# A mixer block with MLP: which engine measures, transposes and orders the first tiles of x

## The chip, the cores and the metric

The kernel runs on one core of one Trainium2 chip. A core has a matrix engine (TensorE, PE in the profile; PEld is its weight load), a vector engine (VectorE, DVE), a scalar engine (ScalarE, ACT), GpSimd (POOL) and a queue engine (SyncE, SP) that issues DMA transfers. The engines run their own instruction streams in order and wait for each other through semaphores. The metric is the device time of one execution in microseconds (us), lower is better; the median of three runs stands for the kernel.

## The reference

```python
B, S, D, F = 1, 2048, 512, 1792          # bf16; w1, w2: D x D; w3: D x F; w4: F x D
def reference(x, w1, w2, w3, w4):
    h = _gelu(_layernorm(x, axis=-1) @ w1)
    c = D // 4
    g0 = jnp.pad(h[:, :, 0*c:1*c], ((0, 0), (1, 0), (0, 0)))[:, :S, :]
    g1 = jnp.pad(h[:, :, 1*c:2*c], ((0, 0), (0, 1), (0, 0)))[:, 1:, :]
    g2 = jnp.pad(h[:, :, 2*c:3*c], ((0, 0), (2, 0), (0, 0)))[:, :S, :]
    g3 = jnp.pad(h[:, :, 3*c:   ], ((0, 0), (0, 2), (0, 0)))[:, 2:, :]
    hs = jnp.concatenate([g0, g1, g2, g3], axis=-1) @ w2
    x1 = x + hs
    h2 = _gelu(_layernorm(x1, axis=-1) @ w3) @ w4
    return x1 + h2
```

Four quarters of the channels of h are shifted along the sequence by 1, -1, 2 and -2 before the second product.

## The kernel before

The 2048 rows are 16 tiles of 128 rows. Row 16p + t lies in tile t, on partition p, so that a shift by one row is, for nearly all rows, a step to the neighbouring tile. The work of a tile of x in the first layer is:

- `st` (line 325, VectorE): statistics of 128x512; `ag` (328, VectorE): mean and variance from them
- `rs` (POOL): a shift of the variance by epsilon (line 349) and a power of -1/2 (358), mostly for two tiles at once
- `norm` (378, VectorE): the normalized tile, `xn`
- the transpose to `xT`: either `tp` (400, four 128x128 transposes on TensorE into PSUM) and then `evA` (412, the eviction by ScalarE), or `dT` (388), one DMA transpose issued by SP. Tiles 0 to 7 go the first way, tiles 8 to 15 the second
- the first product, for pairs p of tiles: pair 0 by input chunk (`m1i`, line 467: 16 matmuls of 256 columns, four chunks of w1 in four steps, so that the first half of w1 is enough to begin), the others by output chunk (`m1`, 451: four matmuls of 256 columns a step)
- `g1` (495, 501, 512, ScalarE): GELU of a pair, into `hT`
- the second product of a tile (`m2`, 526): four matmuls of 512 columns, one for each shifted quarter j, which needs the quarter's neighbouring tile; `add` (538, VectorE) gives x1.

The second layer measures and normalizes tiles of x1 in the order 2, 3, ..., 15, 0, 1 (these are numbers 16 to 31 in the helpers), transposes all of them by DMA (`x1T`), and runs the third product (553) and the fourth (579) in four blocks of 512 rows; a DVE add (593) and a DMA write each output tile.

Every engine's instruction stream is in program order. The order of the first layer's head is written out by hand in the string `HEAD`, whose steps are recorded one after the other (`m1 2 0 3` is pair 2, into PSUM bank 0, output chunk 3; `m2 2 4 0 1` is tile 2, bank 4, quarters 0 and 1; `tp 1 5` is tile 1 into bank 5). The helper then derives the semaphore waits from what each operation reads and writes. An operation that waits holds up all that stands behind it on its engine. The code behind `HEAD` records the rest with helpers for two tiles at a time.

SP issues, in this order: x tiles 0, 1, 2, 3 singly, 4 and 5 together, w1 in two halves, tiles 6 and 7, 8 to 11, 12 to 15, w2, the eight DMA transposes of tiles 8 to 15, w3, twelve transposes of x1, and then w4 in four pieces between the last four. PSUM has eight banks; a step that writes a bank waits until the bank's previous reader is done. Twelve matmuls on constants run at the start and three more when tile 1's statistics are there (`warm`, line 611); they compute nothing that is used.

Of the kernel before, what the change touches and what calls it, by code (L numbers as in the profile page):

```python
# [167 lines left out]
norm 10; g1 3; m2 3 5 0 1 2 3; st 14; ag 12; dT 9; rs 12; st 15; m2 4 6 0 1 2 3; ag 14; ag 15;  # L168
m1 4 0 3; rs 14; dT 11; m1 4 0 1; norm 13; m1 4 0 0; add 3; norm 14; dT 10; m2 5 7 0 1 2 3;
add 2; m1 4 0 2; norm 12; norm 15; dT 13; g1 4; dT 12; dT 14; dT 15  # L170
"""


def bass_standalone__mixer_s_mlp__prompt_kernel(
# [26 lines left out]
    with ExitStack() as es:  # L201
        sb = lambda name, shape, dt: es.enter_context(nc.sbuf_tensor(name, shape, dt))
        x_sb = sb("x_sb", [P, NT, D], BF16)
        x1_sb = sb("x1_sb", [P, NT, D], BF16)
        xT = sb("xT", [P, DC, S], BF16)
# [7 lines left out]
        ident = sb("ident", [P, P], BF16)  # L213
        xn = sb("xn", [P, NXN, D], BF16)
# [14 lines left out]
        pr = Prog()  # L229
# [38 lines left out]
        def load_w4(c, n):  # L268
            g = Gen()
            g_w4.append(g)  # L270
            v = w4.rearrange("(c p) f -> p c f", p=P)
            pr.op("sp", f"w4_{c}", lambda e: e.dma_start(w4_sb[:, c : c + n, :], v[:, c : c + n, :]),
                  w=[g], dma=True)


        def consts():
            g0 = Gen()
            pr.op("pool", "ident0", lambda e: e.memset(ident[:], 0.0), w=[g0])
            g_ident.prev = g0
# [26 lines left out]
        def window(j, t):  # L306

            s = (-1, 1, -2, 2)[j]
            u = t + s
            if 0 <= u < NT:  # L310
                return pos(j, u), [g_h[(j, u // 2)]]
            v = u % NT
            pads = [g_pad[k] for k in g_pad if k in PADS and k[0] == j]
            return pos(j, v) + (-1 if s < 0 else 1), [g_h[(j, v // 2)]] + pads


        def src(q):
# [13 lines left out]
        g_sd = {}  # L331

        def rstd_act(q, n=1):
            g = g_sd[q] = Gen()
# [10 lines left out]
        def rstd_pool(q, n=2, shift=False):  # L345
# [15 lines left out]
            if shift:  # L361
# [2 lines left out]
                                                rstd[:, q : q + n], ALU.mult),  # L364
                      r=[gm] + g_rstd[q : q + n], w=g_nmr[q : q + n])

        def norm(eng, q):
            a, g = src(q)
            s = q % NXN
            g_xn[q] = xn_slot[s].new()  # L370
            if eng == "act":
                pr.op("act", f"norm{q}",
                      lambda e: e.activation(xn[:, s, :], a, ACT_F.Identity,  # L373
                                             bias=nmr[:, q : q + 1], scale=rstd[:, q : q + 1]),
                      r=[g, g_nmr[q], g_rstd[q]], w=[g_xn[q]])
            else:
                pr.op(eng, f"norm{q}",
                      lambda e: e.tensor_scalar(xn[:, s, :], a, mv[:, q, 0:1], rstd[:, q : q + 1],  # L378
                                                ALU.subtract, ALU.mult),
                      r=[g, g_mv[q], g_rstd[q]], w=[g_xn[q]])  # L380
# [25 lines left out]
        def evacT(eng, q):  # L406
            g, b = g_tp[q]
            dst, c = xT_of(q)
            a = ps_bf[:, 1024 * b : 1024 * b + 512].rearrange("p (c s) -> p c s", c=DC)
            o = dst[:, :, P * c : P * (c + 1)]  # L410
            if eng == "act":
                pr.op("act", f"ev{q}", lambda e: e.activation(o, a, ACT_F.Copy), r=[g], w=[g_xT[q]])  # L412
            else:
                pr.op("dve", f"ev{q}", lambda e: e.tensor_copy(o, a), r=[g], w=[g_xT[q]])
# [44 lines left out]
        def mm1_by_input(p, b, dcs):  # L459

            if p not in g_y:
                g_y[p] = ([bank[b + i].new() for i in range(DC)], b)
            for dc in dcs:
                def f(e, dc=dc):
                    for fc in range(DC):
                        dst = ps[:, 512 * (b + fc) : 512 * (b + fc) + 256]
                        ins = e.matmul(dst, w1_sb[:, dc, P * fc : P * (fc + 1)],
                                       xT[:, dc, 256 * p : 256 * (p + 1)],
                                       start=(dc == 0), stop=(dc == DC - 1))
                    return ins  # L470

                pr.op("pe", f"mm1_{p}_1_{dc}", f,
                      r=[g_w[("w1", dc)], g_xT[2 * p], g_xT[2 * p + 1]], w=g_y[p][0])

        def hap(j, p, jn=1):

# [36 lines left out]
                      r=gens, w=[g_h[(j, p)] for j in range(DC)])  # L513


        g_o = {}

        def mm2(t, b, js=(0, 1, 2, 3)):

            if t not in g_o:  # L520
                g_o[t] = (bank[b].new(), b)
            win = [window(j, t) for j in js]

            def f(e):
                for j, (c, _) in zip(js, win):
                    ins = e.matmul(bankap(b), hT[:, j, c : c + P], w2_sb[:, j, :],  # L526
                                   start=(j == 0), stop=(j == DC - 1))
# [76 lines left out]
        def keep_warm(n, b, after=()):  # L604

            g = bank[b].new()
            ones = nc.const_aps.tensor(1.0, (P, 512), BF16)

            def f(e):
                for _ in range(n):  # L610
                    ins = e.matmul(bankap(b), ones[:, 0:P], ones, start=True, stop=True)  # L611
                return ins

            pr.op("pe", f"warm{len(after)}", f, r=list(after), w=[g])
# [37 lines left out]
        def mm2s(k, b):  # L652
            for i in range(2):
                mm2(ORDER2[k + i], b + i)
# [31 lines left out]
        def last_tile():  # L686
# [6 lines left out]

        steps = {
            "st": stats, "ag": aggr, "rs": rstd_pool, "norm": lambda q: norm("dve", q), "tp": peT,
            "evA": lambda q: evacT("act", q), "dT": dmaT,
            "m1i": lambda p, b, *dcs: mm1_by_input(p, b, dcs),
            "warm": lambda n, b, q: keep_warm(n, b, [g_mv[q]]),
            "m1": lambda p, b, *fcs: mm1(p, b, fcs), "g1": gelu1,
            "m2": lambda t, b, *js: mm2(t, b, js), "add": add1,  # L700
        }
# [73 lines left out]
```

## Time and profile before

| what | value |
|---|---|
| median of 3 runs | 138.96 us (138.89 to 139.28) |
| the profiled execution, its own time | 139.09 us |
| its span, first to last instruction | 137.3 us |
| TensorE busy | 131.9 us, 96% of the span |
| VectorE busy | 51.6 us |
| ScalarE busy | 50.0 us |
| POOL busy | 18.3 us |
| first transpose on TensorE | 6.76 us |
| first product (pair 0) | 8.73 us |
| first matmul of the second layer | 38.03 us |
| TensorE's granted clock | 1.00 throughout |

Busy times are summed from the records of single instructions. TensorE's matmuls overlap in the pipeline, and the ends of their records are modelled, so its share says little about idle moments: these are read from the starts of successive matmuls. In a timeline row stand the start, the busy time, engine and line, operation, output and input, shape and count, and in brackets the idle time before it with what ended it.

### The profile page before, as it was taken

The page shows a single profiled execution, that of the slowest core. Times are in us where ns is not written, and L with a number is a line of the kernel's source. Part 1 is how long each engine was busy: PE and PEld are TensorE (multiplying, and loading weights), DVE is VectorE, ACT ScalarE, POOL GpSimd, SP SyncE. Part 2 cuts the span into 40 slices and gives each one's busy share as a digit, 9 for nine tenths or more (in the row PEclk, how much of TensorE's full clock was granted, in tenths as well). Part 3 has the DMA queues.
Part 4 walks back from the last instruction along what each step waited for, and adds up shares of the span by engine and source line. Part 5 has one row for each costly group of instructions (what it writes and reads, how often), then busy time and mean ns, then how long its engine had stood idle before and what let it go on. Part 6 is the DMA issues. An engine that isn't in the chain of part 4 may idle for free.

```text
span 137.3 us, 1790 instructions
## 1 busy us (share of the span) xinstructions
PE 131.9 (96%) x689; PEld 66.5 (48%) x701; DVE 51.6 (38%) x125; ACT 50.0 (36%) x60; POOL 18.3 (13%) x52
## 2 busy tenths in 40 slices
PE   7879999999999999999999999999999999999993
PEld 3267847664444444444444444444444444444452
DVE  0989899999976620000232000023200002232222
ACT  4068622399545555552000555300055530000000
POOL 2542442464312200000000000000000000000000
PEclk9999999999999999999999999999999999999999
DMA  4996144589955599300111100011110001111121
GB/s 106 289 283 238 27 93 82 111 261 351 133 100 113 83 287 257 103 5 0 38 38 38 38 0 5 0 38 38 38 38 0 5 0 38 38 38 38 38 74 41
DMA packets 20119, 12.16 MB, mean 89 GB/s; under 512 B 13712, under 2 KB 19088, under 8 KB 20112
## 3 DMA queue, kind: packets, MB, share of 16 engines
q1 hardware_dynamic: 19968, 12.03, 33.6%
q8 instruction: 5, 0.08, 0.3%
q10 hardware_dynamic: 144, 0.03, 0.1%
q14 instruction: 2, 0.02, 0.0%
HBM read 6.82 MB, written 2.10 MB: 65 GB/s over the span
## 4 chain that ended last, share of the span: by engine, by line
PE 83%; DVE 8%; DMA 4%; POOL 1%; issue 1%; DVEq 0%
PE ps L579 35%; PE ps L553 35%; PE ps L526 8%; PE ps L451 5%; DVE st L325 5%; DVE xn L378 2%; DMA x_sb<-in_x_dram 2%; DMA xT<-xn 2%; POOL rstd L358 1%; DVE mv L328 1%; POOL vpe L349 0%; DVE o_sb L593 0%; DVEq L134 0%
## 5 line engine op out<-in xcount | busy, mean ns | idle before, releaser
L579 PE MATMUL ps<-w_sb,h2T 128*128 128x512 bf16 (+2 forms) x234 | 48.7, 366 | 0.2
L553 PE MATMUL ps<-x1T,w_sb 128*128 128x512 bf16 x219 | 48.6, 379 | 0.3
L566 ACT ACTIVATE h2T<-ps 128x1024 bf16<-128x1024 f32 x28 | 28.6, 1023 | 44.8 <-PE ps L553 44.8
L593 DVE TENSOR_TENSOR o_sb<-ps,x_sb 128x512 bf16<-128x512 f32 (+2 forms) x17 | 11.2, 660 | 75.0 <-PE ps L579 75.0
L579 PEld LDWEIGHTS ps<-w_sb,h2T 128*128 128x128 bf16 x238 | 22.8, 98 | 25.9
L553 PEld LDWEIGHTS ps<-x1T,w_sb 128*128 128x128 bf16 x224 | 21.9, 98 | 26.4
L325 DVE BATCH_NORM_STATS2 st<-x_sb 128x6 f32<-128x512 bf16 x32 | 20.7, 675 | 2.3 <-DMA x_sb<-in_x_dram 2.3
L526 PE MATMUL ps<-w_sb,hT 128*128 128x512 bf16 x61 | 14.3, 379 | 0.2
L451 PE MATMUL ps<-xT,w_sb 128*128 128x256 bf16 x112 | 14.0, 273 | 0.3 <-DMA xT<-xn 0.3
L451 PEld LDWEIGHTS ps<-xT,w_sb 128*128 128x128 bf16 x112 | 10.6, 98 | 3.1 <-issue 0.7
L358 POOL TENSOR_TENSOR rstd<-vpe,neghalf 128x2 f32<-128x2 f32 (+1 forms) x17 | 11.8, 695 | 1.0
L538 DVE TENSOR_TENSOR x_sb<-ps,x_sb 128x512 bf16<-128x512 f32 x16 | 10.3, 678 | 0.3 <-PE ps L526 0.2
L378 DVE TENSOR_SCALAR xn<-x_sb,mv,rstd 128x512 bf16<-128x512 bf16 x22 | 8.3, 405 | 5.2 <-POOL rstd L358 5.0
L526 PEld LDWEIGHTS ps<-w_sb,hT 128*128 128x128 bf16 x64 | 6.2, 98 | 6.3 <-ACT hT L512 0.3
L373 ACT ACTIVATE xn<-x_sb,nmr,rstd 128x512 bf16<-128x512 bf16 x10 | 7.6, 807 | 3.3 <-POOL nmr L363 3.3
L512 ACT ACTIVATE hT<-ps 128x1024 bf16<-128x1024 f32 x6 | 6.1, 1019 | 6.1 <-PE ps L451 6.0
L349 POOL TENSOR_SCALAR vpe<-mv 128x2 f32<-128x2 f32 (+1 forms) x17 | 3.9, 229 | 27.3 <-DVE mv L328 27.2
L412 ACT ACTIVATE xT<-ps 128x512 bf16<-128x512 bf16 x8 | 4.5, 603 | 5.9 <-PE ps L400 5.9
L611 PE MATMUL ps<-const-bfloat16-1.0 128*128 128x512 bf16 x15 | 5.4, 522 | 0.9 <-PEq L760 0.8
L328 DVE BATCH_NORM_AGGREGATE mv<-st 128x2 f32<-128x6 f32 x32 | 4.9, 172 | 0.1
L400 PE MATMUL ps<-ident,xn 128*128 128x128 bf16 x32 | 3.0, 221 | 1.2 <-DVE xn L378 1.2
L611 PEld LDWEIGHTS ps<-const-bfloat16-1.0 128*128 128x128 bf16 x15 | 1.8, 127 | 4.0 <-issue 3.2
(18 smaller groups left out, 12.8 us busy)
## 6 DMA issues: line engine op xcount, KB each, us to landing
w_sb<-in_w_dram SPq DMA_DIRECT2D x4, 512.0 KB, 4.8
out_dram<-o_sb SPq DMA_DIRECT2D x15, 128.0 KB, 1.8
w_sb<-in_w_dram SPq DMA_DIRECT2D x1, 1792.0 KB, 7.3
x_sb<-in_x_dram SPq DMA_DIRECT2D x2, 512.0 KB, 7.5
w_sb<-in_w_dram SPq DMA_DIRECT2D x3, 256.0 KB, 4.1
x_sb<-in_x_dram SPq DMA_DIRECT2D x4, 128.0 KB, 2.5
x_sb<-in_x_dram SPq DMA_DIRECT2D x2, 256.0 KB, 4.1
x1T<-xn SPq DMA_TRANSPOSE x16, 3.6
```

The lines of the kernel that those rows point to most:

```text
L325: pr.op("dve", f"st{q}", lambda e: e.bn_stats(st6[:, q, :], a), r=[g], w=[g_st[q]])
L358: lambda e: e.tensor_tensor(rstd[:, q : q + n], vpe[:, q : q + n], neghalf[:, 0:n], ALU.pow),
L373: lambda e: e.activation(xn[:, s, :], a, ACT_F.Identity, bias=nmr[:, q : q + 1], scale=rstd[:, q : q + 1]),
L378: lambda e: e.tensor_scalar(xn[:, s, :], a, mv[:, q, 0:1], rstd[:, q : q + 1], ALU.subtract, ALU.mult),
L451: ins = e.matmul(dst, w1_sb[:, dc, P * fc : P * (fc + 1)], xT[:, dc, 256 * p : 256 * (p + 1)], start=(dc == 0), stop=(dc == DC - 1))
L526: ins = e.matmul(bankap(b), hT[:, j, c : c + P], w2_sb[:, j, :], start=(j == 0), stop=(j == DC - 1))
L538: lambda e: e.tensor_tensor(x1_sb[:, t, :], bankap(b), x_sb[:, t, :], ALU.add),
L553: ins = e.matmul(bankap(b + i), w3_sb[:, dc, P * fc : P * (fc + 1)], x1T[:, dc, 512 * s : 512 * (s + 1)], start=(dc == 0), stop=(dc == DC ...
L566: pr.op("act", f"g2_{s}_{fp}", lambda e: e.activation(o, a, ACT_F.Gelu_apprx_tanh), r=gens, w=[g])
L579: ins = e.matmul(ps[:, 512 * b : 512 * b + n], h2T[:, fc, s % 2, P * i : P * (i + 1)], w4_sb[:, fc, c0 : c0 + n], start=(fc == 0), stop=(f ...
L593: lambda e: e.tensor_tensor(o_sb[:, s, 0:n], ps[:, 512 * b : 512 * b + n], x1_sb[:, t, c0 : c0 + n], ALU.add),
L611: ins = e.matmul(bankap(b), ones[:, 0:P], ones, start=True, stop=True)
```

## The change

- x tiles 6 and 7 are transposed by DMA, as the first two of now ten transposes of the first layer on SP's queue; their two `tp` and two `evA` are gone.
- Tile 2's statistics come from ScalarE in two passes that sum along the row, `sum` (x) and `dev` ((x - mean) squared), with small POOL steps for the negated mean, for the shifts of tiles 2 and 3 (`vpd`, `vp`) and for the joint power (`pw`). Its `st` and `ag` are gone from VectorE.
- Tile 0 is normalized and transposed first, behind the statistics of tiles 0, 1 and 3; tile 5 is measured between norms 0 and 1. The three later `warm` matmuls stand behind the transpose of tile 0, and eleven instead of twelve lead.
- Pair 0 of the first product goes tile by tile (`m1x`: 32 matmuls of 128 columns instead of 16 of 256).
- Second products of tiles 2 to 7 are recorded as single matmuls, a quarter at a time, in an order of their own between the first products; the first one issued opens the sum and the last closes it, whichever quarter it is.
- Two memsets of constants go from POOL to VectorE; w4 is loaded in two pieces instead of four.

```diff
 HEAD = """
-st 0; ag 0; rs 0 1; st 1; ag 1; rs 1 1; st 2; st 3; ag 2; ag 3; warm 3 3 1; rs 2; norm 1; norm 0;
-tp 1 5; tp 0 4; st 4; evA 1; norm 2; norm 3; evA 0; tp 2 6; tp 3 7; st 5; ag 4; ag 5; m1i 0 0 0;
-evA 3; rs 4; m1i 0 0 1; evA 2; m1i 0 0 2; st 6; m1i 0 0 3; norm 4; m1 1 4 3; norm 5; g1 0;
-tp 4 6; st 7; m1 1 4 0; ag 6; ag 7; tp 5 7; rs 6; evA 4; m1 1 4 1; st 9; evA 5; m1 1 4 2; st 8;
-norm 7; m1 2 0 1; ag 8; ag 9; g1 1; m1 2 0 3; rs 8; norm 6; tp 7 7; st 11; m1 2 0 2; evA 7;
-tp 6 6; norm 8; m1 2 0 0; ag 11; evA 6; m2 2 4 0; m2 2 4 1; st 10; m1 3 2 2; norm 9; ag 10; g1 2;
-m1 3 2 0; rs 10; st 13; m1 3 2 1; m1 3 2 3; st 12; m2 2 4 2; dT 8; m2 2 4 3; norm 11; ag 13;
...
+st 0; ag 0; rs 0 1; st 1; sum 2; st 3; ag 1; ag 3; rs 1 1; norm 0; tp 0 4; dev 2; vpd 2; vp 3;
+evA 0; st 5; warm 3 3 1; norm 1; pw 2 2; tp 1 5; st 4; m1x 0 0 0; ag 5; m1x 0 0 1; norm 3; evA 1;
+m1x 0 0 2; norm 2; ag 4; tp 3 7; m1x 0 0 3; rs 4; m1x 1 0 0; st 6; evA 3; tp 2 6; m1x 1 0 1;
+m1x 1 0 2; st 7; ag 6; evA 2; m1x 1 0 3; ag 7; rs 6; norm 4; g1 0; m1 1 4 0; norm 5; tp 4 6;
+m1 1 4 2; tp 5 7; norm 6; evA 4; m1 1 4 3; evA 5; st 9; m1 1 4 1; st 8; m1 2 0 3; ag 9; ag 8;
+rs 8; m1 2 0 0; norm 7; g1 1; m1 2 0 2; st 13; m1 2 0 1; m2 3 5 0; st 11; m2 2 4 0; dT 6; norm 8;
+m2 5 7 2; m2 2 4 1; g1 2; m2 2 4 2; st 10; ag 11; m2 3 5 2; ag 10; m2 3 5 1; rs 10; norm 9;
+m2 4 6 2; dT 7; m2 5 7 0; m2 2 4 3; st 12; m1 3 2 1; m2 4 6 0; st 14; m2 3 5 3; norm 11; ag 13;
+dT 8; m1 3 2 3; add 2; m1 3 2 2; norm 10; ag 12; m1 3 2 0; ag 14; m2 6 4 2; rs 12; dT 9;
+m2 4 6 1; m2 6 4 0; st 15; ag 15; g1 3; m1 4 0 0; rs 14; m1 4 0 2; norm 13; m2 6 4 1; dT 11;
...
 """
-            pr.op("pool", "eps", lambda e: e.memset(eps_c[:], LN_EPS), w=[g_eps])
-            pr.op("pool", "nh", lambda e: e.memset(neghalf[:], -0.5), w=[g_nh])
+            pr.op("dve", "eps", lambda e: e.memset(eps_c[:], LN_EPS), w=[g_eps])
+            pr.op("dve", "nh", lambda e: e.memset(neghalf[:], -0.5), w=[g_nh])
...
+        def sum_act(q):
...
+            pr.op("act", f"sq_sum{q}",
+                  lambda e: e.activation(sink[:], a, ACT_F.Identity, accum_out=tot[:, q, 0:1]),
+                  r=[g], w=[gs, g_sum[q]])
+            pr.op("pool", f"nm{q}",
+                  lambda e: e.tensor_scalar(nmean[:, q : q + 1], tot[:, q, 0:1], -1.0 / D, None,
+                                            ALU.mult),
+                  r=[g_sum[q]], w=[g_nm[q]])
+        def dev_act(q):
...
+            pr.op("act", f"sq_dev{q}",
+                  lambda e: e.activation(sink[:], a, ACT_F.Square, bias=nmean[:, q : q + 1],
+                                         scale=1.0, accum_out=tot[:, q, 1:2]),
+                  r=[g, g_nm[q]], w=[gs, gd])
...
+        def mm1_tile_by_input(t, b, dc):
...
+            def f(e):
+                for fc in range(DC):
+                    o = 512 * (b + fc) + P * (t % 2)
+                    ins = e.matmul(ps[:, o : o + P], w1_sb[:, dc, P * fc : P * (fc + 1)],
+                                   xT[:, dc, P * t : P * (t + 1)],
+                                   start=(dc == 0), stop=(dc == DC - 1))
+                return ins
...
-                for j, (c, _) in zip(js, win):
+                for n, (j, (c, _)) in enumerate(zip(js, win), n0):
                     ins = e.matmul(bankap(b), hT[:, j, c : c + P], w2_sb[:, j, :],
-                                   start=(j == 0), stop=(j == DC - 1))
+                                   start=(n == 0), stop=(n == DC - 1))
...
-        keep_warm(12, 3)
+        keep_warm(11, 3)
...
-        mm2s(4, 4)
+        mm2(6, 4, (3,))
+        mm2(7, 5, (1, 3,))
...
-            load_w4(2 * (k - 10), 4)
+            if k < 14:
+                load_w4(7 * (k - 10) // 2, 7)
         wide(0, [2, 3])
-        load_w4(12, FC - 12)
```

More of the change, by code (lines that the diff above doesn't have):

```diff
@@ L160 @@
 HEAD = """
-st 0; ag 0; rs 0 1; st 1; ag 1; rs 1 1; st 2; st 3; ag 2; ag 3; warm 3 3 1; rs 2; norm 1; norm 0;
-tp 1 5; tp 0 4; st 4; evA 1; norm 2; norm 3; evA 0; tp 2 6; tp 3 7; st 5; ag 4; ag 5; m1i 0 0 0;
-evA 3; rs 4; m1i 0 0 1; evA 2; m1i 0 0 2; st 6; m1i 0 0 3; norm 4; m1 1 4 3; norm 5; g1 0;
-tp 4 6; st 7; m1 1 4 0; ag 6; ag 7; tp 5 7; rs 6; evA 4; m1 1 4 1; st 9; evA 5; m1 1 4 2; st 8;
-norm 7; m1 2 0 1; ag 8; ag 9; g1 1; m1 2 0 3; rs 8; norm 6; tp 7 7; st 11; m1 2 0 2; evA 7;
-tp 6 6; norm 8; m1 2 0 0; ag 11; evA 6; m2 2 4 0; m2 2 4 1; st 10; m1 3 2 2; norm 9; ag 10; g1 2;
-m1 3 2 0; rs 10; st 13; m1 3 2 1; m1 3 2 3; st 12; m2 2 4 2; dT 8; m2 2 4 3; norm 11; ag 13;
-norm 10; g1 3; m2 3 5 0 1 2 3; st 14; ag 12; dT 9; rs 12; st 15; m2 4 6 0 1 2 3; ag 14; ag 15;
-m1 4 0 3; rs 14; dT 11; m1 4 0 1; norm 13; m1 4 0 0; add 3; norm 14; dT 10; m2 5 7 0 1 2 3;
-add 2; m1 4 0 2; norm 12; norm 15; dT 13; g1 4; dT 12; dT 14; dT 15
+st 0; ag 0; rs 0 1; st 1; sum 2; st 3; ag 1; ag 3; rs 1 1; norm 0; tp 0 4; dev 2; vpd 2; vp 3;
[8 more added lines that the diff above has]
+m2 4 6 1; m2 6 4 0; st 15; ag 15; g1 3; m1 4 0 0; rs 14; m1 4 0 2; norm 13; m2 6 4 1; dT 11;
+m2 4 6 3; add 3; m1 4 0 1; norm 12; norm 15; m1 4 0 3; m2 5 7 1; dT 10; norm 14; m2 7 5 2;
+m2 5 7 3; m2 7 5 0; g1 4; dT 13; dT 12; dT 15; dT 14
 """
@@ L213, in bass_standalone__mixer_s_mlp__prompt_kernel @@
         ident = sb("ident", [P, P], BF16)
+        sink = sb("sink", [P, D], BF16)
+        tot = sb("tot", [P, NT, 2], F32)
         xn = sb("xn", [P, NXN, D], BF16)
@@ L329, in aggr @@
                   r=[g_st[q]], w=[g_mv[q]])
-        g_sd = {}
+        g_sd, g_sum, g_nm, g_dev = {}, {}, {}, {}
+        g_vp = [None] * NT
+        sink_slot = Slot()
         def rstd_act(q, n=1):
@@ L365, in rstd_pool, with vpe_dev, vpe_bn, pow2 @@
                       r=[gm] + g_rstd[q : q + n], w=g_nmr[q : q + n])
+        def sum_act(q):
+            a, g = src(q)
+            g_sum[q], g_nm[q] = Gen(), Gen()
+            gs = sink_slot.new()
+            pr.op("act", f"sq_sum{q}",
[6 more added lines that the diff above has]
+        def dev_act(q):
+            a, g = src(q)
+            gs, gd = sink_slot.new(), Gen()
+            pr.op("act", f"sq_dev{q}",
+                  lambda e: e.activation(sink[:], a, ACT_F.Square, bias=nmean[:, q : q + 1],
+                                         scale=1.0, accum_out=tot[:, q, 1:2]),
+                  r=[g, g_nm[q]], w=[gs, gd])
+            g_dev[q] = gd
+        def vpe_dev(q):
+            g_vp[q] = Gen()
+            pr.op("pool", f"vpe{q}",
+                  lambda e: e.tensor_scalar(vpe[:, q : q + 1], tot[:, q, 1:2], 1.0 / D, LN_EPS,
+                                            ALU.mult, ALU.add),
+                  r=[g_dev[q]], w=[g_vp[q]])
+        def vpe_bn(q):
+            g_vp[q] = Gen()
+            pr.op("pool", f"vpe{q}",
+                  lambda e: e.tensor_scalar(vpe[:, q : q + 1], mv[:, q : q + 1, 1], LN_EPS, None,
+                                            ALU.add),
+                  r=[g_mv[q]], w=[g_vp[q]])
+        def pow2(q, n):
+            pr.op("pool", f"pow{q}",
+                  lambda e: e.tensor_tensor(rstd[:, q : q + n], vpe[:, q : q + n],
+                                            neghalf[:, 0:n], ALU.pow),
+                  r=g_vp[q : q + n] + [g_nh], w=g_rstd[q : q + n])
         def norm(eng, q):
@@ L375, in norm @@
                       r=[g, g_nmr[q], g_rstd[q]], w=[g_xn[q]])
+            elif q in g_nm:
+                pr.op(eng, f"norm{q}",
+                      lambda e: e.tensor_scalar(xn[:, s, :], a, nmean[:, q : q + 1],
+                                                rstd[:, q : q + 1], ALU.add, ALU.mult),
+                      r=[g, g_nm[q], g_rstd[q]], w=[g_xn[q]])
             else:
@@ L457, in mm1 @@
                   w=[gens[h] for h in range(2) if any(fc // 2 == h for fc in fcs)])
-        def mm1_by_input(p, b, dcs):
+        def mm1_tile_by_input(t, b, dc):
+            p = t // 2
             if p not in g_y:
                 g_y[p] = ([bank[b + i].new() for i in range(DC)], b)
[L463 to L473, printed above, removed]
+            def f(e):
[5 more added lines that the diff above has]
+                return ins
+            pr.op("pe", f"m1x_{t}_{dc}", f, r=[g_w[("w1", dc)], g_xT[t]], w=g_y[p][0])
         def hap(j, p, jn=1):
@@ L513, in gelu1 @@
                       r=gens, w=[g_h[(j, p)] for j in range(DC)])
-        g_o = {}
+        g_o, n_o = {}, {}
         def mm2(t, b, js=(0, 1, 2, 3)):
@@ L521, in mm2 @@
                 g_o[t] = (bank[b].new(), b)
+                n_o[t] = 0
+            n0 = n_o[t]
+            n_o[t] += len(js)
             win = [window(j, t) for j in js]
             def f(e):
-                for j, (c, _) in zip(js, win):
+                for n, (j, (c, _)) in enumerate(zip(js, win), n0):
                     ins = e.matmul(bankap(b), hT[:, j, c : c + P], w2_sb[:, j, :],
-                                   start=(j == 0), stop=(j == DC - 1))
+                                   start=(n == 0), stop=(n == DC - 1))
                 return ins
@@ L695, in bass_standalone__mixer_s_mlp__prompt_kernel @@
             "st": stats, "ag": aggr, "rs": rstd_pool, "norm": lambda q: norm("dve", q), "tp": peT,
-            "evA": lambda q: evacT("act", q), "dT": dmaT,
-            "m1i": lambda p, b, *dcs: mm1_by_input(p, b, dcs),
-            "warm": lambda n, b, q: keep_warm(n, b, [g_mv[q]]),
+            "evA": lambda q: evacT("act", q), "evD": lambda q: evacT("dve", q), "dT": dmaT,
+            "warm": lambda n, b, q: keep_warm(n, b, [g_mv[q]]), "sum": sum_act, "dev": dev_act,
+            "vpd": vpe_dev, "vp": vpe_bn, "pw": pow2, "m1x": mm1_tile_by_input,
             "m1": lambda p, b, *fcs: mm1(p, b, fcs), "g1": gelu1,
```

## The prediction

> **What bounds the kernel now.** I read the chain of waits first, in order of time.
>
> ```profile
> 0.73 2.56 DMA x_sb<-in_x_dram
> ...
> 3.31 0.71 DVE st L325
> ...
> 16.56 0.65 DVE st L325 x2
> 17.20 2.48 DMA xT<-xn
> 19.68 0.14 issue
> 19.82 1.47 PE ps L451 x12
> ...
> 128.89 6.04 PE ps L579 x41
> 134.93 0.02 issue
> 134.96 0.29 DVE o_sb L593
> ```
>
> Up to 17.20 us the chain runs through VectorE (measuring and normalizing tiles of x), then through one DMA transpose, and from 19.82 us it is TensorE to the end: no other engine appears before the last add. So every idle moment of TensorE is paid in full, wherever it lies, and nothing else is. Next, TensorE's timeline where it has holes (start, busy time, then in brackets the idle time before):
>
> ```profile
> 5.46 0.81 PE L611 MATMUL ps<-const-bfloat16-1.0 128*128 128x512 bf16 x3
> 6.76 0.72 PE L400 MATMUL ps<-ident,xn 128*128 128x128 bf16 x8 [0.48 <-DVE xn L378]
> 8.18 0.72 PE L400 MATMUL ps<-ident,xn 128*128 128x128 bf16 x8 [0.70 <-DVE xn L378]
> 8.73 0.49 PE L467 MATMUL ps<-xT,w_sb 128*128 128x256 bf16 x3
> ...
> 17.25 2.32 PE L526 MATMUL ps<-w_sb,hT 128*128 128x512 bf16 x10
> 19.82 0.38 PE L451 MATMUL ps<-xT,w_sb 128*128 128x256 bf16 x2 [0.25 <-DMA xT<-xn]
> ```
>
> A matmul's record ends about 0.16 us after the array can take the next one, so I count idle time from start to start, with the spacing of matmuls in an unbroken run: 56 ns at 128 columns, 109 ns at 256, 216 ns at 512. From the first transpose (6.76) on, the holes are 0.09 (between the transposes of tiles 1 and 0), 0.86 (until norm 2), 0.09, 0.15 (12.72 to 12.87, eviction of tile 5) and 0.42 (19.41 to 19.82, transpose of tile 9): 1.61 us. That is nearly all there is to win behind 6.76. Third, the DMA transposes (ns on SP's queue, min/median/max; then us to landing):
>
> ```profile
> L388 SPq DMA_TRANSPOSE xT<-xn x8: 1189/1267/1637, 15.5 to 25.3; - x8
> DMA to landing us min/median/max: 2.5/2.5/3.5
> ```
> ```profile
> L388 SPq DMA_TRANSPOSE x1T<-xn x16: 1194/1265/2207, 28.1 to 50.4; - x16
> DMA to landing us min/median/max: 2.5/3.6/6.3
> ```
>
> One takes SP about 1.31 us, start to start, and 2.5 us to land; behind a bulk load it takes up to 6.3.
>
> **Part 1: the first transpose.** Before, norm 1 starts at 6.32, behind four measurements and four aggregates. After, norm 0 stands behind three of each, since tile 2 went to ScalarE: one measurement (0.58 from start to start) and one aggregate (0.11) less, 6.32 - 0.69 = 5.63. Its scale is ready at 5.20 (POOL's 4.62 + 0.58), so it doesn't wait. Norm 0 takes 0.38, the transpose follows 0.05 later: 6.06, against 6.76. Gain 0.70. The two memsets that move from POOL to VectorE (0.10 each) run before 1.1 us, while VectorE waits for x until 3.31: free. But the three warming matmuls, which lay in the wait before the first transpose (5.46 to 6.27), now stand behind it on TensorE: 3 x 0.216 = 0.65 lost. The eleven leading ones end earlier, in idle time.
>
> **Part 2: tile 2 on ScalarE.** Two passes over 128x512 with a sum as second output; the trace has none. The nearest row is ScalarE's norm of the same shape (807 ns); bounds 0.6 (the eviction of 128x512, 603 ns) and 1.0 (the 128x1024 pass, 1.02 us). I take 0.81. Tile 2 lands at 4.2 (issued 1.65, 2.5 to landing): sum 4.2 to 5.0, POOL's negated mean behind the first power 5.2 to 5.4, second pass 5.5 to 6.3. POOL then does tile 1's power (5.92 to 6.50), two shifts (0.23 each) and the joint power (0.71): 7.74. Norm 3 is due on VectorE at 7.88, so 0.14 is left, and a shorter pass wins nothing, for the shifts stand behind tile 1's power until 6.50. At 1.0 a pass the second ends at 6.6, the joint power at 7.94, and norm 3 slips by 0.17. ScalarE's first eviction, queued behind these passes, needs the first transpose's end (6.45), later than 6.3. Cost zero, at the upper bound 0.2.
>
> **Part 3: tile 5 between norms 0 and 1.** Tiles 4 and 5 land at 6.2 (2.59 + 3.6), VectorE's queue stands until then, and norm 1 starts at 6.3 + 0.58 = 6.9, though its scale is ready at 6.5. Transpose 1 starts at 7.33; the warming matmuls end at 6.93: hole 0.40. Behind norm 1 come measurement 4, an aggregate and norm 3 (7.88 to 8.29), so the transpose of tile 3 starts at 8.34, where the array is free at 8.23 after twelve m1x matmuls: hole 0.11. The eviction of tile 2 (transposed 9.0 to 9.4, behind tile 3's eviction) ends at 10.04; TensorE is through with m1x at 9.91 and needs it at once: hole 0.19. Weight halves w1 landed at 6.9 and 7.6, in time.
>
> **Part 4: the products.** 32 products of 128 columns replace 16 of 256. At 56 ns (the spacing in a run of transposes, and in the last 14 second products, which have this shape) they cost 32 x 0.056 = 1.79 against 16 x 0.109 = 1.75: +0.05. [...]
>
> **Part 5: tiles 6 and 7.** Eight transposes leave TensorE: 8 x 0.056 = 0.45 gained. Two evictions leave ScalarE; two transposes join SP's queue, 2.6 us of it. From 10.10 TensorE has tile pair 1 (16 x 0.109), two transposed tiles (0.45) and pair 2 (1.75): 14.05. Then come ten single second products, which need w2; it landed at 14.2 (5.51 + 8.7): hole 0.25. They last 2.16, until 16.5, where the products of tiles 6 and 7 begin. SP can issue tile 6's transpose when norm 6 is done (POOL's power from 10.5, norm to 11.8), tile 7's after norm 7 at 13.5; landing 13.5 + 2.5 = 16.0, 0.5 ahead of need. If tile 7 took the 3.5 of the slowest first-layer row, 0.5 would be lost; I take 2.5, as most rows have it; 3.5 bounds the forecast, and the far row, behind a bulk load, is a rival below. The rest of the queue: tile 8 at 15.0, tile 9 at 16.3 (lands 18.8, needed 19.3), 10 lands at 21.4 (needed 22.3), 12 at 24.2 (24.7), 14 at 26.8 (28.2); single products of tiles 4 to 7 lie between, so the 0.42 at 19.41 goes. w3 is issued at 25.6 instead of 26.6, since the queue starts 3.7 us earlier and has 2.6 us more in it. VectorE, busy for all 4.30 us from 15.5 to 19.8, has 0.69 less to do, so that it reaches the second layer's statistics, on which the queue's next transposes hang, about a microsecond earlier too. The order of the single products changes only which of them opens and closes its sum: no instruction more. w4 in two pieces issues after 43 us for a use after 60: nothing.
>
> **Sum.** Earlier start -0.70, warming +0.65, work -0.45 + 0.05, holes (0.40 + 0.11 + 0.19 + 0.25 = 0.95 against 1.61) -0.66: -1.11 us. The profiled execution took 139.09 (span 137.3 and 1.8 around it); the median is 138.96. Forecast 138.96 - 1.1, rounded: **137.9**. Its own range is 137.5 to 138.4, by tile 7's upper bound (0.5 more) and by the hole before the second transpose, which goes if tiles 4 and 5 land earlier (0.4 less).
>
> **Rivals.**
>
> *w2 is late.* Before, w2 had 0.8 us of slack (needed at 15.07); now none, and ten products in a row need it. For: the trace shows a 16 KB instruction packet of 1.4 us on the DMA engines at 15.3, when TensorE has started 97 matmuls; after, that count falls near 13.5, while w2 still flows. Against: it is one of 16 engines, and most are through with w2 by then. If hit, w2 lands 1.1 later: 139.0, no change. Chance 0.13.
>
> *The second layer waits for its transposes.* Before, the fourth x1T transpose landed at 37.5 (32.24 + 5.2), TensorE came at 38.03. After, TensorE comes at 36.9. For: these four queue behind w3's load. Against: w3 is issued a microsecond earlier. If they land where they did, 0.6 is lost: 138.5. Chance 0.10.
>
> *Tile 7's transpose is stuck behind the bulk loads* (the slower side). Tile 6's transpose is issued at 11.8, 2.4 us before w2 has landed, on the same queue. Transposes issued behind w3's load landed after 4.6 to 6.3, not 2.5. At the 5.2 of the fourth of them, tile 7 lands at 18.7 and TensorE stands from 16.5 to 18.8: 137.9 + 2.3 = 140.2. The break-even is a landing at 17.5. Against: w2 ends 0.7 after tile 7's issue, whereas w3 had 7 us to go. Chance 0.08.
>
> [...] Chance 0.03. [...]
>
> *The change does not do what it says*: if tiles 4 and 5 land half a microsecond later than in this execution, norm 1 waits and the earlier start is worth little: 138.4. Chance 0.04; the landing is the same load, in the same place of SP's queue.
>
> **How the numbers follow.** The forecast holds the remaining 0.62. A difference of 0.3% (0.42 us) is about what a measurement of this kernel can tell. Faster by more than that (below 138.54): forecast, second layer, late tiles 4 and 5, 0.76. Within it: late w2 and slow products, 0.16. Slower (above 139.38): tile 7 stuck, 0.08. The range from 137.4 to 139.0 takes in all but part of the late w2 and tile 7's case.
>
> **What would show it.** First transpose near 6.1; holes of 0.4 before the second one, 0.2 before tile pair 1 and 0.2 before the first second product; m1x 56 ns apart; from 14.3 no hole until the second layer, whose first product starts near 36.9; last matmul 1.1 us earlier. The forecast is wrong if TensorE stands before the products of tiles 6 and 7, before w2, or at the start of the second layer, by over 0.3 us.

## The result, and the profile after

The changed kernel took 140.33 us (median of 7 runs, 139.5 to 140.91) against 138.96 us (7 runs): ratio 1.0097, 95% interval 1.0075 to 1.0119. It is 1% slower, where 137.9 was forecast. Ratios here and below leave out executions over 1.5% above the fastest of their kernel (one of e2, three of e12); medians and ranges hold them all.

One execution was profiled, with a time of 140.91 us. Its page, and the span from the page's head:

```profile
span 139.1 us, 1806 instructions
...
PEclk9977999999999999999999999999999999999999
```

The row of the granted clock has two sevens, where the row of before had nines throughout. (The row counts as full what lies ahead of the first clock record, 4.43 us in before and 5.52 here; there the leading warming matmuls start 0.43 us apart, not 0.22, so the 1.00 in the table of before holds from 4.43 us on.) The windows view, core 0, one row to a microsecond (busy time and count of each engine, then granted clock, DMA share, GB/s) places them:

```profile
8.00:9.00 1.00, 0.62 (x8) 0.45 (x9) 1.00 (x4) 0.51 (x1) 0.09 (x1) 0.97 1.03 356
9.00:10.00 1.00, 1.00 (x13) 0.96 (x11) 0.40 (x2) 0.09 (x1) 0.43 (x2) 0.50 0.96 343
10.00:11.00 1.00, 1.00 (x13) 1.00 (x11) 0.84 (x2) 0.41 (x1) 0.51 (x1) 0.50 1.01 396
```

In this execution TensorE ran at half clock from 8.94 to 12.35 us, 3.41 us long. The 128-column products and transposes in it started 107 ns apart instead of 56; all in all it cost 1.59 us. TensorE's timeline for the stretch that the prediction worked out, and behind it:

```profile
6.02 0.40 PE L457 MATMUL ps<-ident,xn 128*128 128x128 bf16 x4 [0.40 <-DVE xn L435]
6.25 0.81 PE L671 MATMUL ps<-const-bfloat16-1.0 128*128 128x512 bf16 x3
8.06 0.40 PE L457 MATMUL ps<-ident,xn 128*128 128x128 bf16 x4 [0.99 <-DVE xn L435]
8.78 1.35 PE L525 MATMUL ps<-xT,w_sb 128*128 128x128 bf16 x12 [0.33 <-DMA w_sb<-in_w_dram]
...
24.06 1.03 PE L586 MATMUL ps<-w_sb,hT 128*128 128x512 bf16 x3
25.29 1.92 PE L508 MATMUL ps<-xT,w_sb 128*128 128x256 bf16 x16 [0.20 <-DMA xT<-xn]
```

The first transpose came at 6.02, as forecast (6.06). From then on, from start to start: 1.16 before the second transpose (0.40 forecast), 0.49 before the first products (none forecast), 0.28 at 14.84, 0.36 at 24.93. The chain of waits (start, us, what) no longer turns to TensorE at 19.8 us, but at 25.3:

```profile
4.05 6.08 DMA x_sb<-in_x_dram
10.15 1.29 DVE st L329 x2
...
21.89 3.35 DMA xT<-xn
25.29 1.92 PE ps L508 x16
```

And the DMA transposes of the first layer:

```profile
L445 SPq DMA_TRANSPOSE xT<-xn x10: 1188/1270/2612, 13.4 to 27.2; - x10
...
DMA to landing us min/median/max: 2.4/2.5/3.8
```

Tile 6's was issued at 13.4, not 11.8: tiles 6 and 7 had landed at 10.13 (4.05 + 6.08), not at 8.55. One of the ten, tile 8's, held SP's queue for 2612 ns and landed after 3.75. The first matmul of the second layer started at 39.82 and the last of all at 136.49; 38.03 and 134.70 before.

So there are three suspects: the half clock (A), loads that land later than in the profile of before (B), and something that disturbs a DMA transpose (C). At 17.35 us, 0.74 after the issue of tile 8's transpose, the trace has the first 16 KB packet of an instruction queue (q8 on the page), 1.49 us long. Before, that packet started at 15.32, just ahead of the first transpose (issued 15.52). In this execution it cost TensorE nothing: after the half clock TensorE came so late that no product waited for tile 8 or 9. The 0.36 at 24.93 stands behind tile 10's transpose (issued 21.89), which landed after 3.35 us; an 8 KB packet of a second instruction queue (q14) began at 23.86 us, 1.97 after its issue.

### The profile page after: what moved, and what is told of

Same layout as the page of the kernel before. It is cut to its first block, busy times and chain, and to the rows that moved or that the text cites. A ratio compares the mean times of both kernels' runs of the same rounds, so it can differ in the third digit from the quotient of the medians.

```text
span 139.1 us, 1806 instructions
## 1 busy us (share of the span) xinstructions
PE 133.3 (96%) x696; PEld 68.0 (49%) x708; DVE 50.9 (37%) x125; ACT 50.6 (36%) x62; POOL 19.0 (14%) x52
## 4 chain that ended last, share of the span: by engine, by line
PE 80%; DMA 7%; DVE 7%; SPq 2%; POOL 1%; issue 1%; DVEq 0%
PE ps L639 35%; PE ps L613 35%; PE ps L586 7%; DMA x_sb<-in_x_dram 4%; PE ps L508 4%; DVE st L329 4%; DMA xT<-xn 2%; DVE xn L435 2%; SPq L259 2%; POOL rstd L364 1%; DVE mv L332 1%; SPq L266 1%; DVE x_sb L598 0%; POOL vpe L355 0%; DVE o_sb L653 0%
## 5 line engine op out<-in xcount | busy, mean ns | idle before, releaser
L329 DVE BATCH_NORM_STATS2 st<-x_sb 128x6 f32<-128x512 bf16 x31 | 20.0, 680 | 4.1 <-DMA x_sb<-in_x_dram 4.1
L364 POOL TENSOR_TENSOR rstd<-vpe,neghalf 128x2 f32<-128x2 f32 (+1 forms) x16 | 11.1, 696 | 0.9
L469 ACT ACTIVATE xT<-ps 128x512 bf16<-128x512 bf16 x6 | 3.5, 605 | 3.6 <-PE ps L457 3.6
L525 PE MATMUL ps<-xT,w_sb 128*128 128x128 bf16 x32 | 3.6, 288 | 0.3 <-DMA w_sb<-in_w_dram 0.3
```

Of the source, the lines that this page charges most:

```text
L329: pr.op("dve", f"st{q}", lambda e: e.bn_stats(st6[:, q, :], a), r=[g], w=[g_st[q]])
L364: lambda e: e.tensor_tensor(rstd[:, q : q + n], vpe[:, q : q + n], neghalf[:, 0:n], ALU.pow),
```

## The experiments

All times are medians; before took 138.90, 138.94 and 138.89 us in the three sets of runs (23, 30 and 35 runs).

**e1: the changed kernel once more,** no edit.

> The changed kernel once more, unedited. Theory A (the clock): TensorE idles too much between its warming matmuls and the first products, so its clock falls back to half for one 3.4 us stretch; then this profile shows such a stretch again, with first products 0.11 us apart instead of 0.056, and 139.5 to 140.9 us. Theory B (late loads): x tiles 4 and 5 and the first half of w1 landed late in the profiled execution (6.97 and 8.74 us against 6.23 and 6.91 before) and the new order hangs on them; then the holes before the second transpose and before the first product follow their landings in this profile as well, whatever the clock does.

Measured: 140.2 us (139.79 to 140.45), ratio 1.0092 (1.0067 to 1.0118). In this profile the granted clock was full from 6.52 us on, and the time was no better. Its timeline of TensorE:

```profile
12.45 2.85 PE L508 MATMUL ps<-xT,w_sb 128*128 128x256 bf16 x24
...
19.48 0.82 PE L586 MATMUL ps<-w_sb,hT 128*128 128x512 bf16 x3
21.66 1.03 PE L508 MATMUL ps<-xT,w_sb 128*128 128x256 bf16 x8 [1.36 <-DMA xT<-xn]
```

A hole of 1.53 us from start to start lies before the products of tiles 8 and 9, and it waits for a DMA transpose. The chain of waits names it, tile 9's, 4.14 us from issue to landing:

```profile
17.39 4.14 DMA xT<-xn
21.66 1.03 PE ps L508 x8
```

The packet lay at 19.14 us for 0.93. The DMA view of two windows, 12.94 to 15.4 us (two transposes in flight, no packet) and 19 to 20 us (with it), shows q1 without it and with it (q1 holds the transposes; packets, MB, share of 16 engines' time):

```profile
q1 hardware_dynamic: 600, 0.18, 32.2%
...
q1 hardware_dynamic: 264, 0.06, 165.2%
q8 instruction: 1, 0.02, 5.8%
```

In the first window, which also has the end of w2's load, a packet of q1 takes 0.322 x 16 x 2.46 us / 600 = 21 ns on average; while the instruction packet is there, 1.652 x 16 x 1 us / 264 = 100 ns. The mean is not the common case: in the single records the median is 18 ns in both windows, and 16 of the 264 packets, which took 0.88 to 1.62 us, make the difference.

**e2: more warming matmuls,** 13 ahead and 6 behind the first transpose.

```diff
-evA 0; st 5; warm 3 3 1; norm 1; ...
+evA 0; st 5; warm 6 3 1; norm 1; ...
-        keep_warm(11, 3)
+        keep_warm(13, 3)
```

> The changed kernel with thirteen leading warming matmuls instead of eleven and six instead of three behind the first transpose: TensorE is kept busy to about 7.6 us. Theory A: no half-clock stretch after the first products begin, 1.4 to 1.6 us less than the changed kernel, so about 138.8. Theory B: nothing but the holes' contents change, 140.3.

Measured: 140.13 us (138.88 to 141.07), ratio 1.006 (1.0028 to 1.0091), granted clock full (0.999 or more) in all ten executions. Again 1.56 us of hole at 20.08, tile 9's transpose landing after 4.17, the packet at 19.12. The half clock is not what makes the median slow. Three of the ten took 138.88 to 139.09, about as long as before; only one execution (140.27) was profiled, so what was different in them is not shown.

**e3: tile 5 measured behind the transpose of tile 1.**

```diff
-evA 0; st 5; warm 3 3 1; norm 1; pw 2 2; tp 1 5; st 4; ...
+evA 0; warm 3 3 1; norm 1; pw 2 2; tp 1 5; st 5; st 4; ...
```

> The changed kernel with tile 5 measured behind norm 1 instead of ahead of it. Theory B: the second transpose no longer waits for tiles 4 and 5 and starts near 7.1; what is won is at most the 0.7 of that hole, and nothing where the first half of w1 lands after 8 us, so 139.7 to 140.3. Theory A: TensorE's idle time only moves, the half-clock stretch stays, 140.3.

Measured: 139.98 us (139.15 to 140.39), ratio 1.0067 (1.0039 to 1.0096). The holes before 9 us fell to 0.32, 0.15, 0.24 and 0.26 (in e1 the one before the second transpose alone was 0.94). Part of that is the earlier landing of tiles 4 and 5, 6.19 against 7.04. e1's VectorE shows the wait itself: it measures tile 5 at 7.07, as it lands, and norm 1 follows at 7.67. The packet came at 14.73: tile 6's transpose landed after 4.21, tile 7's after 2.95, and a hole of 0.44 stood at 16.98, before their products. This profile is the fastest of the eight executions (139.15); what the slower ones waited for is not on record.

**e4: the kernel before with the changed kernel's warming pattern** (11 ahead, 3 behind its first transpose).

```diff
-... ag 2; ag 3; warm 3 3 1; rs 2; norm 1; norm 0;
-tp 1 5; tp 0 4; ...
+... ag 2; ag 3; rs 2; norm 1; norm 0;
+tp 1 5; warm 3 3 1; tp 0 4; ...
-        keep_warm(12, 3)
+        keep_warm(11, 3)
```

> The kernel before with only the warming of the changed kernel: eleven leading matmuls, the three later ones behind its first transpose. Theory A: it shows the half-clock stretch too and takes 140 us or more. Theory B: it stays at 139.0, the three late ones costing at most 0.65 us (139.6).

Measured: 138.99 us, ratio 1.0018 (0.9993 to 1.0043), full clock in nine of ten executions (0.988 in the other, 140.01). In its profile, at full clock, tiles 4 and 5 landed at 6.86, w1 at 7.52 and 8.87, tiles 6 and 7 at 9.56, all later than in the first profile of before, and the time was the same: the kernel before has room for that. Not for any landing: its third transpose stands behind the measurement of tile 4, and in e12 below, where that tile landed at 7.25, the hole there is 1.42 instead of 0.86.

**e5, e6, e8: the packet moved by dummy code.** In e5, 44 dummy matmuls of 128 columns lead in place of 11 of 512: the same columns in all, but 33 more matmuls with their weight loads ahead in TensorE's program. e6 has 16 more (6 of 512 and 21 of 128), e8 is the kernel before with 33 more.

```diff
                 for _ in range(n):
                     ins = e.matmul(bankap(b), ones[:, 0:P], ones, start=True, stop=True)
+                for _ in range(0 if after else 44):
+                    ins = e.matmul(bankap(b)[:, 0:P], ones[:, 0:P], ones[:, 0:P],
+                                   start=True, stop=True)
...
-        keep_warm(11, 3)
+        keep_warm(0, 3)
```

> The changed kernel, its eleven leading warming matmuls of 512 columns replaced by 44 of 128: the same array time, but 33 more matmuls with their weight loads ahead of the work in TensorE's program. Theory C (the program's next 16 KB): TensorE's instruction stream is fetched in packets of 16 KB by the DMA engines that carry the transposes; in the second profile of the changed kernel such a packet at 19.1 us made tile 9's transpose land 4.1 us after its issue instead of 2.5, and TensorE stood 1.5 us before the products of tiles 8 and 9. With 33 matmuls more the packet is due near 11 us, ahead of the first transpose: transposes land after 2.5, the 1.5 us hole is gone, about 138.7. Theory B (late loads): the holes before the second transpose and the first product stay, and with them 140.2.

> The same with 16 matmuls more instead of 33 (six of 512 columns and 21 of 128). Theory C: the packet is due near 13 to 15 us and meets the transposes of tiles 6 and 7; the hole moves in front of the products of tiles 6 and 7 and is smaller, since these have 0.5 us to spare and the ten single second products ahead of them: 139.3 to 139.8. Theory B: 140.2.

> The kernel before with the same 33 more matmuls: its packet came at 15.3 us, just ahead of its first transpose at 15.5, and now comes near 11.5. Theory C: nothing to win, 138.8 to 139.0. If the smaller warming matmuls themselves change the time, it shows here.

Measured: e5 138.86 us (137.99 to 139.49), ratio 0.999 (0.9963 to 1.0017); e6 139.16, ratio 1.0009 (0.9986 to 1.0032); e8 138.75, ratio 0.9985 (0.9956 to 1.0015). In e5 the packet lay at 13.12, when only the first transpose (issued 12.88) was under way. e5's timeline of TensorE, the same rows as those of e1:

```profile
12.40 2.85 PE L508 MATMUL ps<-xT,w_sb 128*128 128x256 bf16 x24
...
19.42 0.82 PE L586 MATMUL ps<-w_sb,hT 128*128 128x512 bf16 x3
20.08 1.04 PE L508 MATMUL ps<-xT,w_sb 128*128 128x256 bf16 x8
```

and the landing of its ten transposes:

```profile
DMA to landing us min/median/max: 2.4/2.5/3.3
```

At 12.4 us e1 and e5 stand within 0.05 us of each other, at 19.4 within 0.06; then e1 waits 1.5 us and e5 doesn't. The medians differ by 140.2 - 138.86 = 1.34. The same 33 dummies make 138.94 - 138.75 = 0.19 in the kernel before, where there was little to remove. In e6 the packet came at 13.23, ahead of the first transpose (13.58), and not among those of tiles 6 and 7 as I had expected: no product waits for a transpose in its timeline. In these three nothing but TensorE's code was changed, and the packet moved 2.7 to 6 us earlier. That q8 carries TensorE's program, as theory C has it, is my reading of that; no view names the engine, nor shows whether the DMA engines that carried the packet carried the transposes. The packet's time alone would not say so, for with the same TensorE code it lay at 17.35, 19.14 (after, e1) and 14.73 (e3), and what moved it there is not known. The count of matmuls started by then says more: 96 to 117 with the dummies (e5, e6, e8), 94 to 132 in the six profiles without; had the dummies not mattered to the packet, its count would have gone up by the 33 or 16.

**e7, e11: both, code ahead and tile 5 later,** with 33 and with 28 more matmuls (e7: 44 of 128 columns and none of 512; e11: 39 and 1), and e3's order.

> The 33 more matmuls and tile 5 measured behind norm 1. If theory C explains the 1.5 us hole and theory B the early holes (0.5 of them by tile 5's place), both are won: 138.2 to 138.4, faster than both kernels. By theory B alone 140.0.

> The changed kernel with 28 more dummy matmuls ahead and tile 5 measured behind the transpose of tile 1. In e7 (33 more) the first packet came at 11.6 us, ahead of the DMA transposes, and the second at 26.8, where it caught the transpose of tile 14 (hole 0.76). With five fewer both should come later by 0.5 to 1 us: the first near 12.2, still ahead of the first transpose, the second near 27.6, behind the landing of the last one of the first layer. Theory C (packet) and B (landings) together: no hole over 0.3 us behind 13 us, 138.2 us (137.9 to 138.5). Without the packet's effect: 138.9 as e7. If the second packet still catches tile 14 or 15: 138.9.

Measured: e7 138.88 us, ratio 0.999 (0.9975 to 1.0006), where 138.2 to 138.4 was expected; e11 138.65 (138.29 to 139.56), ratio 0.9992 (0.9966 to 1.0017). In e7 the first packet lay at 11.58, before all transposes, and the second, which before comes at 35 us, at 26.80. Its timeline:

```profile
26.89 1.89 PE L586 MATMUL ps<-w_sb,hT 128*128 128x512 bf16 x8
29.38 1.38 PE L508 MATMUL ps<-xT,w_sb 128*128 128x256 bf16 x11 [0.60 <-DMA xT<-xn]
```

The transpose issued last before it (24.94) landed after 4.39, and the hole is 0.76 from start to start. e11's packets came at 12.08 and 27.77, the second as the last transpose landed (27.88): behind 9 us no hole over 0.18 but single missing records. Against e3, the same order without dummies, e11 gains 139.98 - 138.65 = 1.33, as much as e5 against e1. The time expected of e11 (137.9 to 138.5) was missed by 0.15: the first products waited 0.53 for w1's second half, which landed at 8.58.

**e9, e10: without the load of w1's second half,** on e5 and on the kernel before. The products that should read it read the first half a second time, so these two kernels do the same work on less data and don't compute the reference.

```diff
-        load_w("w1", w1_sb, w1, 2, 2)
...
-                        ins = e.matmul(dst, w1_sb[:, dc, P * fc : P * (fc + 1)],
+                        ins = e.matmul(dst, w1_sb[:, dc % 2, P * fc : P * (fc + 1)],
```

> The changed kernel with 33 more dummy matmuls ahead (as in e5), and without the load of w1's second half: the products that read it read the first half again, so the load and its landing at 8.9 to 9.7 us are left out of the computation. Theory B (the landings in the head decide what is left after the packet is out of the way): the hole of 0.98 us before the third step of pair 0 goes, half of it comes back as waits behind it (evictions, tile 3's transpose), so about 138.4 us (138.1 to 138.6), against 138.86 for e5; x tiles 6 and 7 land about 1 us earlier. Rival (what is left after the packet is not in the head but in the transposes of tiles 6 to 15 or in the second layer): 138.9 as e5.

> The kernel before without the load of w1's second half (its products read the first half again; the load is left out). Theory B: the kernel before has room in its head, since its first product starts at 8.7 us behind four transposes, so 138.9 us (138.7 to 139.1), no change. Rival: if it too gains 0.3 or more, the late landings cost both kernels the same and don't explain why the change wins nothing.

Measured: e9 138.42 us, ratio 0.9969 (0.9947 to 0.9991); e10 138.60, ratio 0.9987 (0.9965 to 1.001). Both fell: e9 by 0.44 against e5, from another set of runs and with intervals that overlap; e10 by 0.29 against before, where no change was expected, with an interval that takes in none. That doesn't tell the theories apart. e9's time is in the expected range, but not by the expected way, for the hole did not go in its profile. In e5 it stood before the third step, for the second half; in e9 it stands before the first step, since the first half now landed as late as 8.57. e5, then e9, timelines of TensorE:

```profile
7.59 0.61 PE L525 MATMUL ps<-xT,w_sb 128*128 128x128 bf16 x8
9.01 0.40 PE L525 MATMUL ps<-xT,w_sb 128*128 128x128 bf16 x4 [0.82 <-DMA w_sb<-in_w_dram]
```
```profile
7.51 0.40 PE L457 MATMUL ps<-ident,xn 128*128 128x128 bf16 x4 [0.31 <-DVE xn L435]
8.62 0.84 PE L525 MATMUL ps<-xT,w_sb 128*128 128x128 bf16 x12 [0.71 <-DMA w_sb<-in_w_dram]
```

**e12: the kernel before with five dummies fewer,** to move its packet into its own transposes.

```diff
-... ag 2; ag 3; warm 3 3 1; rs 2; ...
+... ag 2; ag 3; rs 2; ...
-        keep_warm(12, 3)
+        keep_warm(10, 3)
```

> The kernel before with five dummy matmuls fewer (10 instead of 12 lead, and the three later ones are gone). Their work lay in idle time. Theory C: TensorE reaches the point at which the next 16 KB of its program are fetched about 0.8 us later, so the packet falls at 15.9 to 16.5 us instead of 15.3, behind the issue of the first DMA transpose (15.5): the transposes of tile 8 or 9 land 3.6 to 4.2 us after issue instead of 2.5, the hole of 0.42 us before the products of tile 9 grows to 1.2 or more, and the kernel takes 139.7 to 140.3 us. Theory B: no change, 138.9. Theory A (clock): if the longer pause ahead of the first transpose lets the clock drop to half for a stretch, the granted clock of the profile shows it below 0.995, and the time is up by as much as 1.5.

Measured: 139.99 us (138.52 to 141.01), ratio 1.0052 (1.0019 to 1.0085), with a granted clock of 0.975 to 0.988 in 8 of 12 executions. The packet moved to 16.89 and tile 8's transpose landed after 3.65, as theory C has it. But the clock row has sevens here, and TensorE was 1.53 us late in pair 0 for it, so late that the transposes were there in time:

```profile
PEclk9977999999999999999999999999999999999999
```

In this profile the time is the clock's and the late landing's (tiles 4 and 5 at 7.25) and not the packet's; as a test of C by its time the run is spoilt. The four executions at full clock took 138.52, 139.12, 140.74 and 141.01, too few to say more.

**Taken together.** The 14 profiles hold 130 first-layer transposes, each with its issue and landing, and the packets of the instruction queues. Of the 93 with no instruction packet under way between 0.9 and 2.4 us after issue, 91 landed after 2.39 to 2.56 us; the two others (2.70, 2.99) came right behind a disturbed one. All 22 that took 3.2 us or more had a packet start 0.36 to 2.11 us after issue. With eight of them it was q8's 16 KB; the other 14 met an 8 KB packet of another instruction queue (q14) that started between 22.3 and 23.9 us in each profile. One of these is the slowest row of before, 3.48. When in a transpose the packet comes matters: all 20 in which one began 0.74 to 2.11 us after issue took 3.2 us or more, but of the twelve with one at 0.36 to 0.66 only two did; the other ten landed after 2.53 to 2.95.

## Why the prediction was wrong

**Transposes at 2.5 us each (Part 5): wrong, and the largest miss.** "I take 2.5, as most rows have it", and tile 9 "lands 18.8, needed 19.3", so that "the 0.42 at 19.41 goes". Most rows do have 2.5, in the changed kernel too. But before, the queue of transposes began 0.2 us behind the packet's start, so the trace showed transposes with that packet out of the way: the first, issued while it was there, took 2.76, the next three 2.48 to 2.49. The change starts the queue at 13 us and leaves the packet among them, and one lands after 3.75 to 4.2. In e1 the hole is 1.53 instead of none, out of 2.3 us between the forecast -1.11 and the measured +1.2. I had the packet in hand, in the rival on w2, and asked only what it would do to w2: nothing, in none of the profiles did the first second product wait for it. I placed it "near 13.5"; it lay at 17.35, 19.14 and 19.12 in the changed kernel and in e2. Shown by e5 (1.34 us) with e1's and e5's timelines, and by the landings; e11 against e3 gains as much (1.33), though e3's one profile shows only 0.44 of it.

**Landings from one profile (Part 3): wrong.** "Tiles 4 and 5 land at 6.2"; "weight halves w1 landed at 6.9 and 7.6, in time"; tiles 6 and 7 at 8.55. The issues are at the same 2.59, 3.06, 3.54 and 4.05 us in all of these profiles, the landings aren't:

| profile | tiles 4, 5 | w1, first half | w1, second half | tiles 6, 7 |
|---|---|---|---|---|
| before | 6.23 | 6.91 | 7.60 | 8.55 |
| e4 (before, warming moved) | 6.86 | 7.52 | 8.87 | 9.56 |
| e8 (before, +33) | 6.62 | 8.22 | 9.11 | 9.79 |
| after | 6.97 | 8.74 | 9.43 | 10.13 |
| e1 (after again) | 7.04 | 7.70 | 8.98 | 9.68 |
| e5 (after, +33) | 6.27 | 6.96 | 8.97 | 9.62 |
| e6 (after, +16) | 6.68 | 7.35 | 9.63 | 10.32 |

The profile of before was the earliest of them in every column, and of all 14 in every column but the first (6.19 in e3), leaving aside e9 and e10, whose queue has a load less. The hole of 0.40 was 0.94 in e1 and 1.16 in after, and e5's wait of 0.98 for w1's second half was not in the sum at all. I had a late landing as the last rival, at 0.04, and for tiles 4 and 5 alone.

**The sum, with what it measured in e1** (full clock): start -0.61 for -0.70, warming matmuls +0.65, work -0.40, holes 3.18 (0.14 of it the first transposes, at 6.14, ahead of the first clock record at 6.52: a row of 0.56 for four, where the next four, at 8.13, took 0.40) against 1.61, +1.57, where -0.66 was forecast. That makes +1.21, and the last matmul did start 1.19 later than before (135.89 against 134.70). Of the other holes, the one before tile pair 1 was sized well: 0.18 (0.19). The 0.11 forecast before tile 3's transpose didn't come, since TensorE had already lost 0.21 waiting for w1's second half (8.98); that a hole of 0.11 stands before tile 4's transpose instead is a coincidence. The first second product didn't wait for w2 (0.25 forecast): TensorE came at 15.14 instead of 14.05, and w2 had landed at 13.75 instead of 14.24. The same sum for e5: start -0.85, warming +0.65, work -0.40, holes 1.85 - 1.61 = +0.24, together -0.36, measured -0.39. So with the packet away the change wins 0.39 in that profile and 0.08 by the medians, with an interval that takes in no gain, and not 1.1. What is missing in the profile is the waits for loads in the head: 0.56 and 0.98, where 0.40 was forecast. That these landings are the cause rests on the timelines; e9 and e10 left open how much each load holds.

**The 128-column products: right.** 56 ns apart at full clock (eight from 9.47 to 9.92 in e5). No run shows a slower spacing at full clock, for which the forecast held 0.03; in after they started 107 ns apart, at a granted clock of 0.50.

**Tile 7's transpose behind the bulk loads: the right time by a wrong way.** That rival gave 140.2, but tile 7's landed after 2.42 in after and 2.43 in e1. **The half clock** was in no rival. It was there in one of 11 executions of the changed kernel, which was the profiled one, and cost 1.59 there; the kernel's other ten took 139.5 to 140.48 without it.

**Is a better version in sight?** e11 has the lowest median of those that compute all of it, 138.65, but its ratio to before (0.9966 to 1.0017) tells it from none.

## What to carry to other kernels

Work that is moved in time also moves against what stays. Here the first layer's DMA transposes began at about 13 us instead of 15.5, and a 16 KB instruction packet (q8), which before began at 15.32, ahead of them, lay among them at 17.35 to 19.14 (after, e1, e2); one transpose landed after 3.75 to 4.2 us instead of 2.5. 33 and 16 more dummy matmuls ahead (e5, e6) put the packet at 13.12 and 13.23. So read the instruction queues' packets beside the issues and landings, and try a few dummy instructions: it is the cheapest way to see whether a hole is the order's fault or the packet's. And where a sum spends the slack of a load, take its landing from several profiles, not from one: tiles 6 and 7 landed at 8.55 to 10.32 in the table above.

## What the runs showed of the hardware that was not expected

- Where an instruction packet (16 KB, 0.92 to 1.49 us where it met transposes; 8 KB, 0.31 to 1.02 us) began 0.74 to 2.11 us after the issue of a DMA transpose, the transpose landed after 3.2 to 4.39 us instead of 2.5, in all 20 cases. The first 16 KB packet came when 90 to 132 matmuls had started (counted in the records, of which a few are missing), the second 101 to 150 matmuls later. In after TensorE's own matmuls show no pause at the packet (17.35, 1.49 long): the second products from 17.08 on start 0.216 apart through it. What waited in e1, 1.53 us, were the products of a late transpose. How a packet delays a transpose is not shown. On record are e1's 16 packets of q1 that took 0.88 to 1.62 us while q8's was there, against a median of 18 ns, and how the landings look: the trace has 16 updates of a semaphore for each transpose. In ten of the 22 transposes that took 3.2 us or more fifteen updates came on time, by 2.58 us, and one alone came late (in after, for tile 10, 2.56 and 3.35 us; in e7, for tile 14, 2.48 and 4.39); in the other twelve all 16 came late together (in after, for tile 8, 3.58 to 3.75). Why it is the one or the other is open.
- The half-clock stretch in after and in e12 was 3.41 us long and began 3.41 us after the first record of a full clock. By the windows view TensorE was busy for 1.70 of the 3.41 us that went before in after (5.52 to 8.94) and 1.13 in e12 (5.34 to 8.75), shares of 0.50 and 0.33. In the other twelve profiles the clock stayed full, and the shares of the first 3.41 us on record were 0.55 (e11), 0.58 (e9), 0.61 (e5) and up to 0.99 (e2). Since the ends of matmuls are modelled, these shares are rough. That idle time sets off the half clock, as theory A has it, is not shown.
- A row sum as ScalarE's second output is an instruction of its own, 0.18 to 0.19 us behind the pass of 0.63 to 0.72; together 0.82 and 0.90, where the forecast took 0.81.
